# A gated S4 and feed-forward kernel: the order of the first projection's opening steps, with nine rounding steps moved between two engines

## The chip, the cores and the metric

The kernel runs on one NeuronCore of a Trainium2 chip. The metric is the device time of one execution in microseconds (us), the median of several runs. Five engines work side by side, each through its own list of instructions in order: TensorE (PE, with its weight loads as PEld), VectorE (DVE), ScalarE (ACT), GpSimd (POOL) and SyncE (SP, which here only issues transfers). They wait for one another through semaphores.

## The reference

The input `A_u` has 2048 rows of 512 features. It is normalized row by row, and two branches read the result:

```python
xn = _layernorm(x, axis=-1)
s = _A_ref(xn, A_re, A_im, B_re, B_im, C_re, C_im, log_dt, Dskip)   # S4: K from exp(dt*A*l), convolution by FFT
h = _gelu(xn @ w1 + b1)                                             # 512 -> 1792, tanh form
g = _silu(h @ w2 + b2)                                              # 1792 -> 512
return x + s * g
```

In `_A_ref` the parameters give for every feature a kernel `K` of 2048 taps as a sum over 128 states of complex exponentials. Everything is float32.

## The kernel before

**Tiling.** The feed-forward branch goes in steps `(v, f)`: `v` counts blocks of 512 rows (four blocks, visited twice, `v` 0 to 7), `f` counts 14 tiles of 128 hidden features, seven of them in each visit. Step number 0 to 55 stands in the names below. Each float32 matrix product is made of three fp32r products: a matrix is split into a rounded high part and a low remainder, and high times high, high times low and low times high are added up. `w1h`, `w1l`, `w2h`, `w2l` are the parts of the weights, `xh`, `xl` those of the normalized and transposed rows, `hh`, `hl` those of the gelu's result.

**One step** consists of the first projection (`first_half`, 12 matmuls with 512 columns, lines 255 to 257, in two halves; step 0 uses `first_start`, line 265), the gelu on ACT (`gate`, line 269), its rounded copy on ACT (`gate_high`, line 275), the remainder on DVE (`ffn_rest`, line 281) and the second projection (`second_part`, four quarters of three matmuls, lines 294 to 296; step 0 adds `b2` in two of the quarters with one more matmul each, line 293, from the tile `b2r`). The weights come by `stage_first` (a tile of `w1`, line 221) and `stage_second` (a tile of `w2`, line 226) into four rotating buffers; `split` makes the high parts on ACT (line 238) and the low parts on DVE or POOL (line 240).

**Beside it**, the S4 kernel `K` is generated in 32 subblocks. `params` computes on POOL, DVE and ACT the parameters of a quarter of the features (lines 499 to 574, with an arctan at line 520); `gen_phase` (PE, line 598) and `gen_round` (ACT, line 606, or DVE, line 608) and `gen_wrap` (DVE, line 612) make the phases, `gen_sin` the sines on ACT, `gen_size` the magnitudes on POOL (line 623), `gen_tables` the products on DVE (lines 646 to 653), and `gen_sum` sums them on PE (line 662, 128 small matmuls). `gen_round(s, h, other)` is on ACT where `h != other`, else on DVE.

**The order** is written by hand. `prologue()` loads the first rows, normalizes them (`ln_stats`, line 325, `ln_rsqrt`, lines 335 to 345, `ln_scale`, line 350), transposes them on PE (line 366), casts them on ACT (line 375) and DVE (line 381) and runs step 0's first projection. Ahead of the transposes PE runs 31 `warm` matmuls on an identity (line 432). Then a string `ORDER` of 1250 tokens is walked: `F.j.h` is half `h` of step `j`'s first projection, `G`, `H`, `R` its gelu, copy and remainder, `S.j.i` quarter `i` of its second projection, `W.f` and `WB.f` the loads of `w1` and `w2`, `WS.f.k` the splits (`k` 0 and 1 the high parts of `w1` and `w2`, 2 and 3 the low parts, on POOL where a 1 follows), `P.b` the next piece of `params(b)`, `LL`, `LS`, `LR`, `LC`, `LD` load, statistics, root, scaling and storing of later rows, `TF`, `TH`, `TL` their transposes, `A.s.h`, `B.s.h`, `C.s.h` phase, rounding and wrapping of subblock `s`, `Z`, `N`, `E`, `Q` magnitudes, sines, products and sums. Every engine gets its instructions in the order of these tokens, so a token that waits holds up everything later on the same engine.

The functions that the diff touches, and what calls them:

Of the kernel before, what the change touches and what calls it, by code (L numbers as in the profile page):

```python
# [48 lines left out]
WS.0.3 P.0 LD.0 P.0 P.0 WS.1.0 WS.1.1 WS.1.2 F.1.0 G.0 H.0 LD.1 W.2 R.0 WS.1.3 F.1.1 WS.2.0 LS.2.0 G.1  # L49
H.1 LS.3.1 LS.3.0 S.0.0 S.0.1 S.0.2 WB.2 WS.2.1 LL.4 WS.2.2 R.1 WS.2.3 LS.2.1 P.0 P.0 F.2.0 F.2.1 LL.5  # L50
W.3 WS.3.0 WB.3 W.4 WB.4 WS.3.1 WS.3.2 W.5 F.3.0 F.3.1 P.0 P.0 G.2 G.3 P.0 P.0 P.0 P.0 S.0.3 H.2 R.2 H.3
WS.4.0 WS.3.3 WS.4.1 WS.4.2 WS.5.0 LR.2 S.1.0 WB.5 LC.2 S.1.1 S.1.2 S.1.3 S.2.0 S.2.1 P.0 W.6 F.4.0
F.4.1 S.2.2 LC.3 S.2.3 KL.0.0 KL.0.1 G.4 H.4 R.3 TF.2.0 TH.2.0 KL.1.0 KL.1.1 S.3.0 Z.0 A.0.0 B.0.0.1
LS.5.0 R.4 TF.2.1 TH.2.1 BB S.3.1 TL.2.0 TF.3.0 WB.6 C.0.0 A.0.1 P.0 WS.5.1 WS.4.3.1 S.3.2 Z.1 TL.2.1
TH.3.0 B.0.1 WS.6.0 WS.5.2 F.5.0 TL.3.0 WS.6.1 C.0.1 N.0.0 N.0.1 TF.3.1 F.5.1 G.5 P.1 A.1.0 S.3.3 S.4.0
S.4.1 LS.4.0 LS.5.1 TH.3.1.1 B.1.0 C.1.0 A.1.1 B.1.1 TL.3.1 WS.6.2 S.4.2 S.4.3 H.5 E.0.0 LS.4.1 F.6.0
F.6.1 G.6 H.6 C.1.1 R.5 WS.5.3.1 S.5.0 LR.4 S.5.1 F.7.0 F.7.1 R.6 LC.5 LC.4 KL.2.0 KL.2.1 A.2.0 N.1.0
F.8.0 E.0.1 LK.0 S.5.2 S.5.3 N.1.1 F.8.1 LD.2 G.7 WS.6.3 E.0.2 E.1.0 B.2.0.1 G.8 H.7 LD.3 H.8 S.6.0
O.0.0 P.1 S.6.1 S.6.2 C.2.0 A.2.1 B.2.1 P.1 R.7 R.8 O.0.1 C.2.1 N.2.0 F.9.0 KL.3.0 F.9.1 KL.3.1 G.9
KL.4.0 A.3.0 E.1.1 E.1.2 S.6.3 S.7.0 TF.4.0 Z.2 P.1 Q.1 H.9 S.7.1 O.0.3 O.0.2 S.7.2 B.3.0.1 C.3.0 A.3.1  # L60
P.1 TH.4.0 TL.4.0 N.2.1 S.7.3 KL.4.1 TF.4.1 TH.4.1 R.9 F.10.0 F.10.1 B.3.1.1 S.8.0 Z.3 S.8.1 LD.5 C.3.1
N.3.0 N.3.1 G.10 H.10 E.2.0 A.4.0 KL.5.0 P.1 E.2.1 TL.4.1 E.2.2 B.4.0 C.4.0 R.10 F.11.0 F.11.1 G.11 H.11
S.8.2 E.3.0 S.8.3 S.9.0 R.11 E.3.1 E.3.2 LD.4 LL.6 TF.5.0 TH.5.0 U.1 A.4.1 TL.5.0 D B.4.1 F.12.0 F.12.1
G.12 H.12 S.9.1 C.4.1 S.9.2 LK.1 R.12 Z.4 UD.1 A.5.0 B.5.0.1 C.5.0 TF.5.1 TH.5.1 Q.3 P.1 LL.7 A.5.1 P.1
P.1 S.9.3 S.10.0 S.10.1 S.10.2 S.10.3 KL.6.0 KL.5.1 P.1 U.3 KL.6.1 B.5.1 C.5.1 LS.6.0 S.11.0 S.11.1
S.11.2 P.1 N.4.0 TL.5.1 P.1 F.13.0 F.13.1 LS.7.0 OK.0 N.4.1 E.4.0 S.11.3 N.5.0 N.5.1 UD.3 G.13 H.13 Z.5
S.12.0 E.4.1 E.4.2 E.5.0 S.12.1 A.6.0 LK.2 R.13 S.12.2 S.12.3 Z.6 B.6.0 F.14.0 F.14.1 C.6.0 A.6.1 LS.7.1
P.1 E.5.1 B.6.1 G.14 H.14 C.6.1 F.15.0 KL.7.0 E.5.2 F.15.1 P.2 A.7.0 G.15 LS.6.1 S.13.0 H.15 R.14 R.15
B.7.0.1 N.6.0 N.6.1 S.13.1 C.7.0 S.13.2 S.13.3 Q.5 A.7.1 P.1 F.16.0 F.16.1 B.7.1 F.17.0 F.17.1 LR.6 LC.6
LC.7 P.2 E.6.0 E.6.1 KL.8.0 O.1.0 S.14.0 E.6.2 C.7.1 O.1.2 O.1.1 S.14.1 G.16 H.16 S.14.2 G.17 H.17 N.7.0  # L70
# [1238 lines left out]
```

## Time and profile before

| | |
|---|---|
| time, median of 3 runs | 532.0 us (531.85 to 533.8) |
| profiled execution, its own time | 532.66 us |
| profiled execution, span | 530.8 us |
| granted TensorE clock | 0.997 |
| PE busy | 517.2 us (97%) |
| DVE busy | 428.5 us (81%) |
| ACT busy | 391.6 us (74%) |
| POOL busy | 258.5 us (49%) |

The span is that of the traced instructions; the execution's own time holds 1.86 us more. Times inside the profile are counted from the span's start. PE's busy time is that of pipelined matmuls, so what matters is where PE stood idle and who released it.

### The profile page before, as it was taken

The page shows a single profiled execution, that of the slowest core. Times are in us where ns is not written, and L with a number is a line of the kernel's source. Part 1 is how long each engine was busy: PE and PEld are TensorE (multiplying, and loading weights), DVE is VectorE, ACT ScalarE, POOL GpSimd, SP SyncE. Part 2 cuts the span into 40 slices and gives each one's busy share as a digit, 9 for nine tenths or more (in the row PEclk, how much of TensorE's full clock was granted, in tenths as well). Part 3 has the DMA queues.
Part 4 walks back from the last instruction along what each step waited for, and adds up shares of the span by engine and source line. Part 5 has one row for each costly group of instructions (what it writes and reads, how often), then busy time and mean ns, then how long its engine had stood idle before and what let it go on. Part 6 is the DMA issues. An engine that isn't in the chain of part 4 may idle for free.

```text
span 530.8 us, 16519 instructions
## 1 busy us (share of the span) xinstructions
PE 517.2 (97%) x6995; PEld 421.6 (79%) x6995; DVE 428.5 (81%) x726; ACT 391.6 (74%) x558; POOL 258.5 (49%) x384
## 2 busy tenths in 40 slices
PE   8899999999999999999999999999999999999995
PEld 7677778878777776877777777788889998998882
DVE  6998999999998789787875886898257779677896
ACT  3698896999987987988778799799464573663331
POOL 5629377657697478669818175635301002103041
PEclk9999999999999999999999999999999999999998
DMA  8937438752327974418135533590757539442562
GB/s 223 318 119 217 155 102 254 259 181 77 132 80 226 364 212 143 140 46 235 41 108 175 185 59 112 131 186 34 253 199 228 68 108 216 160 163 82 182 208 94
DMA packets 86087, 85.91 MB, mean 162 GB/s; under 512 B 41751, under 2 KB 60699, under 8 KB 84989
## 3 DMA queue, kind: packets, MB, share of 16 engines
q1 hardware_dynamic: 76944, 66.49, 42.5%
q0 software_dynamic: 8768, 17.83, 10.8%
q8 instruction: 55, 0.90, 0.7%
q10 hardware_dynamic: 300, 0.53, 0.3%
q14 instruction: 20, 0.16, 0.1%
HBM read 51.28 MB, written 33.55 MB: 160 GB/s over the span
## 4 chain that ended last, share of the span: by engine, by line
PE 84%; DVE 6%; ACT 3%; POOL 3%; issue 2%; DMA 2%; POOLq 0%; DVEq 0%; ACTq 0%
PE s L918 11%; PE z L294 9%; PE z L296 8%; PE z L295 8%; PE f L255 8%; PE f L257 8%; PE f L256 8%; PE s L896 6%; PE sa L955 6%; PE kg L662 5%; PE ph L598 3%; PE y L1014 2%; DMA w1s<-in_B_w_dram 1%; DVE hl L281 1%; PE xT L366 1%
## 5 line engine op out<-in xcount | busy, mean ns | idle before, releaser
L623 POOL TENSOR_TENSOR mm<-mm,rc 128x32 f32<-128x32 f32 (+4 forms) x150 | 97.1, 647 | 11.8
L294 PE MATMUL z<-w2h,hh 128*128 128x512 f32 x224 | 95.6, 427 | 0.0
L255 PE MATMUL f<-xh,w1h 128*128 128x512 f32 x220 | 91.6, 416 | 0.2 <-DVE hl L281 0.2
L257 PE MATMUL f<-xh,w1l 128*128 128x512 f32 x220 | 87.1, 396 | 2.8 <-DVE w1l L240 1.5
L296 PE MATMUL z<-w2h,hl 128*128 128x512 f32 x224 | 87.7, 391 | 0.1
L295 PE MATMUL z<-w2l,hh 128*128 128x512 f32 x224 | 87.7, 391 | 0.0
L256 PE MATMUL f<-xl,w1h 128*128 128x512 f32 x220 | 86.8, 395 | 0.0
L612 DVE SCALAR_TENSOR_TENSOR ra<-ra,ph 128x512 f32<-128x512 f32 x64 | 43.8, 684 | 19.6 <-ACT ra L606 18.7
L918 PE MATMUL s<-X,mc 64*64 64x128 f32 x1536 | 58.3, 272 | 0.8 <-DVE t L936 0.4
L936 DVE TENSOR_TENSOR t<-s,uh 128x512 f32<-128x512 f32 x64 | 40.9, 684 | 15.6 <-ACT uh L926 12.1
L269 ACT ACTIVATE f<-f,b1s 128x512 f32<-128x512 f32 x56 | 37.2, 665 | 19.3 <-PE f L257 18.0
L646 DVE TENSOR_TENSOR e<-mm,ra 128x1024 f32<-128x1024 f32 x32 | 43.3, 1355 | 10.1 <-ACT ra L634 4.3
L257 PEld LDWEIGHTS f<-xh,w1l 128*128 128x128 f32 x220 | 41.3, 188 | 12.2 <-DVE w1l L240 2.2
L255 PEld LDWEIGHTS f<-xh,w1h 128*128 128x128 f32 x220 | 41.5, 189 | 10.9 <-issue 1.5
L296 PEld LDWEIGHTS z<-w2h,hl 128*128 128x128 f32 x224 | 42.0, 188 | 10.2 <-DVE hl L281 0.5
L294 PEld LDWEIGHTS z<-w2h,hh 128*128 128x128 f32 x224 | 42.4, 189 | 9.0 <-issue 0.3
L620 POOL COPY mm<-rc 128x32 f32<-128x32 f32 x30 | 14.9, 496 | 71.0 <-DVE e L653 40.9
L918 PEld LDWEIGHTS s<-X,mc 64*64 64x64 f32 x1536 | 44.9, 133 | 5.8 <-issue 2.0
L926 ACT COPY uh<-s 128x512 f32<-128x512 f32 x32 | 18.8, 587 | 40.7 <-PE s L918 24.7
L295 PEld LDWEIGHTS z<-w2l,hh 128*128 128x128 f32 x224 | 42.2, 189 | 8.2
L256 PEld LDWEIGHTS f<-xl,w1h 128*128 128x128 f32 x220 | 41.4, 188 | 9.1
L281 DVE TENSOR_TENSOR hl<-f,hh 128x512 fp32r<-128x512 f32 x56 | 37.8, 682 | 10.6 <-ACT hh L275 10.6
(188 smaller groups left out, 1128.5 us busy)
## 6 DMA issues: line engine op xcount, KB each, us to landing
x<-in_A_u_dram SPq DMA_DIRECT2D x8, 512.0 KB
xs<-x SPq DMA_DIRECT2D x8, 512.0 KB
xt_h<-xh POOLq DMA_DIRECT2D x4, 1024.0 KB, 6.2
xt_l<-xl POOLq DMA_DIRECT2D x4, 1024.0 KB, 8.8
kgd<-ko SPq DMA_DIRECT2D x16, 256.0 KB
za<-zo SPq DMA_DIRECT2D x4, 1024.0 KB
xh<-xt_h POOLq DMA_DIRECT2D x4, 1024.0 KB, 6.6
xl<-xt_l POOLq DMA_DIRECT2D x4, 1024.0 KB, 9.3
```

The source lines that it names most:

```text
L255: PE.matmul(p, wh[:, k, :], xh[:, k, :], start=(k == 0), stop=False)
L256: PE.matmul(p, wh[:, k, :], xl[:, k, :], start=False, stop=False)
L257: PE.matmul(p, wl[:, k, :], xh[:, k, :], start=False, stop=(k == KD - 1))
L281: V.tensor_sub(hl, hf, hh)
L294: PE.matmul(z, hh[:, s], wh, start=(f0 == 0 and not rows), stop=False)
L295: PE.matmul(z, hh[:, s], wl, start=False, stop=False)
L296: PE.matmul(z, hl[:, s], wh, start=False, stop=(f0 == FA - 1))
L612: V.scalar_tensor_tensor(ra[:, 0, c], ra[:, 1, c], MAGIC, p, op0=ALU.subtract, op1=ALU.subtract)
L623: GP.tensor_mul(mv[:, :, 0:3:2, w:2 * w], mv[:, :, 0:3:2, 0:w], rc[:, 2 + 2 * i:4 + 2 * i, :].rearrange("p j c -> p c j").unsqueeze(3).to_ ...
L646: V.tensor_mul(e1, m1.unsqueeze(1).to_broadcast([P, 2, CH, N1]), ra[:, :, :, :N1])
L918: PE.matmul(p[ka * 64:(ka + 1) * 64, r, o, :, jj], w, xf[b][h, c, :, k, :], start=(c == 0), stop=(c == 1), skip_group_check=True)
L936: V.tensor_mul(t, p[:, i, :, 1].unsqueeze(1).to_broadcast([P, 2, 2, P]), uh)
```

## The change

It has three parts.

- `b2`'s low part. `bias_low()`, one DVE subtraction on one row (line 424), is taken out of the prologue, where it stood between the statistics of the first two row tiles, and becomes a token `BL`, placed behind the first half of step 1's first projection.
- The first 217 tokens of `ORDER` are written in another order, about a sixth of the string; none is lost. From the token `TL.4.0` on, the order is the old one.
- Nine roundings change their engine. 14.1, 19.0, 20.1, 22.0, 23.0 and 26.1 go from ACT to DVE, and 6.0, 27.1 and 28.1 go from DVE to ACT. DVE has 34 of the 64 roundings instead of 31.

```diff
 ORDER = """
-WS.0.3 P.0 LD.0 P.0 P.0 WS.1.0 WS.1.1 WS.1.2 F.1.0 G.0 H.0 LD.1 W.2 R.0 WS.1.3 F.1.1 WS.2.0 LS.2.0 G.1
-H.1 LS.3.1 LS.3.0 S.0.0 S.0.1 S.0.2 WB.2 WS.2.1 LL.4 WS.2.2 R.1 WS.2.3 LS.2.1 P.0 P.0 F.2.0 F.2.1 LL.5
+WS.1.0 WS.1.1 WS.0.3 WS.1.2 LD.0 LD.1 F.1.0 P.0 P.0 P.0 G.0 W.2 WB.2 W.3 BL F.1.1 H.0 R.0 S.0.0 S.0.1
+P.0 P.0 WS.1.3 WB.3 S.0.2 S.0.3 G.1 H.1 LS.2.0 LS.3.1 R.1 LS.3.0 WS.2.0 WS.2.1 WS.2.2 WS.2.3 S.1.0 F.2.0
...
-E.17.1 E.17.2 P.3 A.19.0 B.19.0.1 S.31.1 C.19.0 S.31.2 Q.17 A.19.1 P.3 R.33 B.19.1.1 KL.19.1 C.19.1
+E.17.0 N.18.0 H.34 E.17.1 E.17.2 P.3 A.19.0 B.19.0 S.31.1 C.19.0 S.31.2 Q.17 A.19.1 P.3 R.33 B.19.1.1
...
         ln_stats(0, mv[:, 0:2, :])
-        bias_low()
         ln_stats(1, mv[:, 2:4, :])
...
         "BB": bias_spread,
+        "BL": bias_low,
```

**ACT, from the end of the prologue on.** In the names, `w1h_340` (before) and `w1h_313` (now) are the high part of step 1's `w1`, `w1h_369` and `w1h_426` that of step 2, `pr_` tiles belong to `params(0)`, `f_0_1` is step 1's projection and `hh_0`, `hh_1` are the rounded gelus of steps 0 and 1. Before:

```order
L507 ACTIVATE pr_bi<-pr_wr 128x128
L508 ACTIVATE pr_cr<-pr_wi 128x128
L238 CAST w1h_340<-w1s_212 128x512
L238 CAST w2h_342<-w2s_214 128x512
L269 ACTIVATE f_0_0_301<-f_0_0_301,b1s 128x512
L275 CAST hh_0_355<-f_0_0_301 128x512
L238 CAST w1h_369<-w1s_358 128x512
L269 ACTIVATE f_0_1_347<-f_0_1_347,b1s 128x512
L275 CAST hh_1_380<-f_0_1_347 128x512
L238 CAST w2h_371<-w2s_403 128x512
L520 ACT_TABLE_LOAD
L520 ACTIVATE pr_cr<-pr_bi 128x128
```

Now:

```order
L238 CAST w1h_313<-w1s_212 128x512
L238 CAST w2h_315<-w2s_214 128x512
L507 ACTIVATE pr_bi<-pr_wr 128x128
L508 ACTIVATE pr_cr<-pr_wi 128x128
L269 ACTIVATE f_0_0_300<-f_0_0_300,b1s 128x512
L275 CAST hh_0_368<-f_0_0_300 128x512
L520 ACT_TABLE_LOAD
L520 ACTIVATE pr_cr<-pr_bi 128x128
L269 ACT_TABLE_LOAD
L269 ACTIVATE f_0_1_323<-f_0_1_323,b1s 128x512
L275 CAST hh_1_411<-f_0_1_323 128x512
L238 CAST w1h_426<-w1s_355 128x512
```

The casts of step 1's weights went ahead of the two parameter instructions; the arctan, with a table load on either side of it, went ahead of step 1's gelu; and the cast of step 2's `w1` went behind that gelu.

**DVE, behind the transposes of the first rows.** Here `w1l_341` and `w1l_314` are the low part of step 1's `w1`, `w2l_251` and `w2l_250` that of step 0's `w2`. Before:

```order
L240 TENSOR_TENSOR w2l_251<-w2s_137,w2h_250 128x512
L511 TENSOR_TENSOR pr_ci<-pr_bi,pr_cr 128x128
L512 TENSOR_TENSOR pr_br<-pr_bi,pr_cr 128x128
L513 TENSOR_TENSOR pr_m<-pr_cr,pr_bi 128x128
L515 TENSOR_SCALAR pr_bi<-pr_ci 128x128
L516 RECIPROCAL pr_bi<-pr_bi 128x128
L517 TENSOR_TENSOR pr_bi<-pr_bi,pr_br 128x128
L240 TENSOR_TENSOR w1l_341<-w1s_212,w1h_340 128x512
L281 TENSOR_TENSOR hl_0_360<-f_0_0_301,hh_0_355 128x512
```

Now:

```order
L240 TENSOR_TENSOR w2l_250<-w2s_137,w2h_249 128x512
L240 TENSOR_TENSOR w1l_314<-w1s_212,w1h_313 128x512
L511 TENSOR_TENSOR pr_ci<-pr_bi,pr_cr 128x128
L512 TENSOR_TENSOR pr_br<-pr_bi,pr_cr 128x128
L513 TENSOR_TENSOR pr_m<-pr_cr,pr_bi 128x128
L515 TENSOR_SCALAR pr_bi<-pr_ci 128x128
L516 RECIPROCAL pr_bi<-pr_bi 128x128
L517 TENSOR_TENSOR pr_bi<-pr_bi,pr_br 128x128
L424 TENSOR_TENSOR b2r<-b2st,b2r 1x512
L281 TENSOR_TENSOR hl_0_370<-f_0_0_300,hh_0_368 128x512
```

`w1l` of step 1 went ahead of the six parameter instructions, and `b2r` took its old place.

**DVE, a little later.** `w1l_370` (before) and `w1l_427` (now) are the low part of step 2's `w1`, `hl_1` is the remainder of step 1's gelu, `bst` and `mv` are statistics of rows. Before:

```order
L325 BN_STATS bst_0_385<-x_228 128x6
L326 BN_AGGR mv_374<-bst_0_385 128x2
L240 TENSOR_TENSOR w1l_370<-w1s_358,w1h_369 128x512
L281 TENSOR_TENSOR hl_1_409<-f_0_1_347,hh_1_380 128x512
L240 TENSOR_TENSOR w2l_372<-w2s_403,w2h_371 128x512
```

Now:

```order
L281 TENSOR_TENSOR hl_1_421<-f_0_1_323,hh_1_411 128x512
L325 BN_STATS bst_0_423<-x_228 128x6
L326 BN_AGGR mv_413<-bst_0_423 128x2
L240 TENSOR_TENSOR w1l_427<-w1s_355,w1h_426 128x512
L240 TENSOR_TENSOR w2l_429<-w2s_357,w2h_428 128x512
```

Step 2's `w1l` went behind step 1's remainder and one pair of statistics. Further on, the low part of step 3's `w1` (`WS.3.2`) stands behind the parameter instructions of lines 534 to 550, ahead of which it stood.

On SP the loads of row tiles 4 and 5 (`LL.4`, `LL.5`), which stood ahead of the loads of `w1` of step 3 and of all later ones, now stand behind `w1` and `w2` of steps 3 and 4.

More of the change, by code (lines that the diff above doesn't have):

```diff
@@ L54 @@
[L54 to L58, printed above, removed]
@@ new lines @@
+P.0 P.0 R.2 LR.2 WS.4.0 WS.3.3 WS.4.1 WS.4.2 F.3.1 S.2.0 LC.2 KL.0.0 S.2.1 S.2.2 S.2.3 WB.5 P.0 LS.5.0
+G.3 F.4.0 F.4.1 H.3 R.3 S.3.0 LS.4.0 A.0.0 WS.5.0 G.4 H.4 B.0.0.1 TF.2.0 R.4 TH.2.0 WS.5.1 WS.4.3.1
+C.0.0 W.6 S.3.1 S.3.2 KL.0.1 WB.6 WS.6.0 TF.2.1 BB TH.2.1 A.0.1 S.3.3 S.4.0 LC.3 KL.1.0 KL.1.1 P.0
+TL.2.0 TF.3.0 TL.2.1 S.4.1 Z.0 B.0.1 C.0.1 WS.5.2 WS.6.1 TH.3.0 WS.6.2 F.5.0 LS.5.1 N.0.0 N.0.1 TL.3.0
+P.1 A.1.0 S.4.2 TF.3.1 B.1.0 F.5.1 G.5 S.4.3 TH.3.1.1 TL.3.1 F.6.0 C.1.0 A.1.1 LS.4.1 E.0.0 H.5 R.5
@@ new lines @@
+A.23.0 B.23.0 S.39.1 S.39.2 N.22.0 N.22.1 S.39.3 S.40.0 C.23.0 A.23.1 B.23.1.1 KL.24.0 KL.25.0 S.40.1
+S.40.2 Q.21 U.21 C.23.1 N.23.0 S.40.3 R.42 E.22.0 E.22.1 Z.23 P.3 N.23.1 S.41.0 S.41.1 S.41.2 A.24.0
+E.22.2 B.24.0.1 F.43.0 E.23.0 F.43.1 C.24.0 G.43 H.43 A.24.1 B.24.1.1 C.24.1 F.44.0 F.44.1 R.43 G.44
+S.41.3 A.25.0 E.23.1 E.23.2 H.44 F.45.0 B.25.0.1 N.24.0 Q.23 C.25.0 A.25.1 R.44 ZL.1 F.45.1 F.46.0
+F.46.1 B.25.1.1 UD.21 KL.26.0 KL.24.1 N.24.1 ZA.1.2 ZA.1.1 ZA.1.3 ZA.1.0 KL.25.1 C.25.1 Z.24 E.24.0
@@ L126 @@
+E.29.2 ZA.2.2 UD.27 A.31.0 B.31.0 ST H.52 Q.29 C.31.0 A.31.1 ZA.2.3 S.49.2 S.49.3 G.53 S.50.0 Z.31
+N.30.0 B.31.1.1 S.50.1 R.52 F.54.0 F.54.1 C.31.1 S.50.2 N.30.1 H.53 E.30.0 S.50.3 U.29 S.51.0 S.51.1
+S.51.2 N.31.0 N.31.1 R.53 F.55.0 E.30.1 S.51.3 E.30.2 E.31.0 E.31.1 KL0 UD.29 S.52.0 S.52.1 F.55.1
+S.52.2 ZG.2 ZD.2 E.31.2 Q.31 S.52.3 S.53.0 S.53.1 S.53.2 S.53.3 G.54 U.31 G.55 H.54 H.55 R.54 R.55 UD.31
 """
```

129 lines of the change are left out of this document (60 added, 69 removed).

## The prediction

> **What bounds the kernel now.** I read first the busy shares on the page, then the list of what PE waited for over the whole span, then the timelines of the first 30 us engine by engine. The shares:
>
> ```profile
> PE 517.2 (97%) x6995; PEld 421.6 (79%) x6995; DVE 428.5 (81%) x726; ACT 391.6 (74%) x558; POOL 258.5 (49%) x384
> ```
>
> PE's waits, longest in total first (us in total, times, longest):
>
> ```profile
> PE f L257 <- DVE w1l L240: 1.5, 1, 1.5
> PE warm L432 <- POOL ident masks.py:199: 1.5, 1, 1.5
> PE f L257 <- issue: 1.3, 1, 1.3
> PE f L265 <- ACT xh L375: 0.7, 1, 0.7
> PE xT L366 <- DVE x L350: 0.5, 1, 0.5
> PE ph L598 <- DVE ra L612: 0.4, 2, 0.2
> ...
> PE xT L366 <- DVE hl L281: 0.2, 1, 0.2
> PE f L255 <- DVE hl L281: 0.2, 1, 0.2
> ```
>
> PE sets the end: it is busy 97% of the span, and its matmuls are the same ones before and after. So a new order is worth just what it takes from PE's waits or adds to them. The change rewrites the front of the kernel, where the first wait lies (step 1's third matmul, 1.5 us for `w1l`) and the 0.5 us ahead of the transposes. PE's timeline there (start, duration, engine, line; in brackets the idle time ahead and its releaser):
>
> ```profile
> 4.56 6.31 PE L432 MATMUL warm<-ident 128*128 128x128 f32 x50
> 11.38 2.17 PE L366 MATMUL xT<-ident,x 128*128 128x128 f32 x16 [0.52 <-DVE x L350]
> 14.22 1.20 PE L265 MATMUL f<-xh,w1h 128*128 128x512 f32 x4 [0.67 <-ACT xh L375]
> ...
> 17.13 0.40 PE L255 MATMUL f<-xh,w1h 128*128 128x512 f32 x1
> ...
> 19.29 0.50 PE L257 MATMUL f<-xh,w1l 128*128 128x512 f32 x1 [1.53 <-DVE w1l L240]
> ...
> 21.73 0.40 PE L293 MATMUL z<-b2r,ones 128*128 128x512 f32 x1
> ```
>
> DVE's:
>
> ```profile
> 6.07 0.18 DVE L326 BATCH_NORM_AGGREGATE mv<-bst 128x2 f32<-128x6 f32 x1
> 6.44 0.70 DVE L424 TENSOR_TENSOR b2r<-b2st,b2r 1x512 fp32r<-1x512 f32 x1 [0.20 <-ACT b2r L421]
> 7.17 0.69 DVE L325 BATCH_NORM_STATS2 bst<-x 128x6 f32<-128x512 f32 x1
> ...
> 10.78 2.06 DVE L350 TENSOR_SCALAR x<-x,mv,rs 128x512 f32<-128x512 f32 x4
> ...
> 15.77 0.68 DVE L240 TENSOR_TENSOR w2l<-w2s,w2h 128x512 fp32r<-128x512 f32 x1
> 16.37 0.28 DVE L511 TENSOR_TENSOR pr_ci<-pr_bi,pr_cr 128x128 f32<-128x128 f32 x1
> ...
> 18.34 0.29 DVE L517 TENSOR_TENSOR pr_bi<-pr_bi,pr_br 128x128 f32<-128x128 f32 x1
> 18.55 0.68 DVE L240 TENSOR_TENSOR w1l<-w1s,w1h 128x512 fp32r<-128x512 f32 x1
> 19.15 0.68 DVE L281 TENSOR_TENSOR hl<-f,hh 128x512 fp32r<-128x512 f32 x1
> ```
>
> And ACT's:
>
> ```profile
> 12.08 2.09 ACT L375 CAST xh<-xT 128x512 fp32r<-128x512 f32 x4 [3.64 <-PE xT L366]
> ...
> 15.55 0.31 ACT L508 ACTIVATE pr_cr<-pr_wi 128x128 f32<-128x128 f32 x1 [1.10 <-POOL pr_wi L504]
> ...
> 17.32 0.66 ACT L269 ACTIVATE f<-f,b1s 128x512 f32<-128x512 f32 x1 [0.43 <-PE f L265]
> 18.02 0.59 ACT L275 CAST hh<-f 128x512 fp32r<-128x512 f32 x1
> 20.77 0.62 ACT L238 CAST w1h<-w1s 128x512 fp32r<-128x512 f32 x1 [2.17 <-DMA w1s<-in_B_w_dram]
> ```
>
> Step 1's `w1l` (DVE, 18.55) is late because six parameter instructions, 16.37 to 18.6, stand ahead of it; and those hang on ACT's line 508, which got `pr_wi` from POOL only at 15.55.
>
> **The change part by part.** PE's pace: ten matmuls from 19.29 to 21.73, 0.24 us each with the refill behind the wait; I use 0.233 for an undisturbed one. Two DVE instructions on 512 columns start 0.60 apart (18.55, 19.15).
>
> *1. `b2r` leaves the first statistics.* It cost DVE the time from 6.17 to 7.17, its own wait included. That is 1.0 us if the second row tile had landed by 6.17; the trace shows only that it had by 7.17, so 0 to 1.0, and I take 1.0. Scaling then starts at 9.78 for 10.78 and its first quarter is done at 10.3. But PE's warm matmuls end at 4.56 + 6.31 = 10.87 whatever DVE does, so the transposes gain only 0.5, and with them the casts (11.6 to 13.7) and step 0's projection (13.74 for 14.22). DVE's low parts follow the casts: `w2l` of step 0 at 15.27 for 15.77.
>
> *2. Step 1's weights ahead of the parameters.* `w1h` is now cast right behind ACT's casts, 13.7 to 14.3. `w1l` follows `w2l` at 15.27 + 0.60 = 15.87 and ends at 16.55. Step 1 starts at 17.13 - 0.48 = 16.65 and wants `w1l` two matmuls later, at 17.1: it is there. The matmul goes at 17.1 instead of 19.29, **-2.2 us**, which holds both the 1.5 and the 0.5.
>
> *3. What is late next.* Ten matmuls on, at 19.44, PE wants `b2r`. DVE's parameters now run from 16.47 to 18.7 and `b2r` behind them to 19.35: no wait, with 0.1 to spare. `hl` of step 0 starts at 19.25 and is wanted at 20.14: no wait. Where this cover fails, each costs what it is late by, some tenths.
>
> *4. Step 2's low part.* ACT now runs the arctan, between two table loads, ahead of step 1's gelu. Both kinds of row:
>
> ```profile
> 23.74 1.28 ACT L520 ACT_TABLE_LOAD   x1
> 25.04 0.31 ACT L520 ACTIVATE pr_cr<-pr_bi 128x128 f32<-128x128 f32 x1
> ```
>
> `hh` of step 0 ends at 18.02 + 0.59 - 0.48 = 18.1; load, arctan and load take 1.30 + 0.31 + 1.30, so the gelu starts at 21.05, and the cast behind it runs from 21.75 to 22.35. DVE waits for that cast: `hl` of step 1 from 22.4, a pair of statistics (0.8) from 23.0, step 2's `w1l` from 23.8 to 24.5. PE: fourteen matmuls of step 0 from 19.44 to 22.7, three of step 1 to 23.4, and the third of step 2, at 23.87, finds `w1l` 0.6 us away. This wait is new: **+0.6**, from 0 (ACT or DVE some tenths ahead) to 1.2.
>
> The Trainium skill, "ScalarE: Activation LUTs", section "What ACT_TABLE_LOAD costs", puts a switch of tables at 1.28 us for the load and 1.38 more for a drain; by it this term would be an estimated 3.4 instead of 0.6. The trace disagrees: the arctan starts 0.02 us after its load ends, with no drain between.
>
> *5. Step 3's low part* now stands behind thirteen parameter instructions, which wait for POOL's line 531. POOL's row, and DVE's first and last of the thirteen:
>
> ```profile
> 25.21 0.46 POOL L531 TENSOR_TENSOR pr_br<-pr_br,pr_m 128x128 f32<-128x128 f32 x1
> ```
>
> ```profile
> 27.33 0.34 DVE L534 SCALAR_TENSOR_TENSOR pr_ci<-pr_ci,sm_dt,pr_br 128x128 f32<-128x128 f32 x1
> ...
> 30.29 0.28 DVE L550 SCALAR_TENSOR_TENSOR xp<-pr_ai,pr_cr 128x128 f32<-128x128 f32 x1
> ```
>
> POOL's chain starts from DVE's line 517, now 0.1 later, so it ends at 25.8. The thirteen take 30.57 - 27.33 = 3.24, to 29.1, and step 3's `w1l` is ready at 29.75. PE finishes step 2's first half at 25.4, nine matmuls of step 1 at 27.5, the other half at 28.9, and wants that `w1l` at 29.4: **+0.4**, from 0 to 0.8.
>
> *6. The later transposes'* wait of 0.2 came from a remainder that stood behind four scalings on DVE; in the new order two of the four come behind it: **-0.2**, from 0 on.
>
> *7. Loads.* The cast of step 2's `w1` waited for its load until 20.77. In the new order it comes behind step 1's gelu, at 22.4, so the weights' earlier place on SP is worth nothing. Row tiles 4 and 5 (1 MB) are now issued when step 2's buffers are free, some 25 to 26.5, and DVE wants them only behind step 3's low parts, after 35. The rate in that stretch, the last column in GB/s:
>
> ```profile
> 20.00:30.00 10.00, 10.00 (x45) 7.90 (x44) 8.57 (x24) 7.18 (x10) 5.12 (x12) 1.00 0.74 243
> ```
>
> 1 MB takes 4.3 us at 243 GB/s: 0. If they were later than 35, DVE would stop ahead of step 3's remainder and PE behind it.
>
> *8. Roundings.* DVE's rows of that kind (ns, least, median and most), and the chain of waits where number 19.0 now comes, ahead of line 612:
>
> ```profile
> L608 DVE TENSOR_SCALAR ra<-ph x31: 671/691/693, 47.2 to 361.3; 128x512 f32<-128x512 f32 x31
> ```
>
> ```profile
> 239.54 0.60 DVE ra L612
> 240.13 0.61 DVE hl L281
> ...
> 240.79 0.50 PE f L255
> ```
>
> PE already waits here for the remainder, so one more DVE instruction ahead of both, 0.6 apart like its neighbours, is **+0.6**. At the other eight places PE has next to no wait, and I take 0; the five that go to DVE could cost 0.6 each (+3.0), and the three that leave it take no listed wait away.
>
> Sum: -2.2 + 0.6 + 0.4 - 0.2 + 0.6 = -0.8. The profiled execution took 532.66, so its like would take 531.9; the median of the runs shown, 532.0, is 0.66 below it, which gives **531.2**. The terms' own bounds make this 530.0 to 532.3.
>
> **The rivals.** *Faster, slack everywhere*: the waits of 4 and 5 are sums of many small gaps and may not come, and the chain ahead of 19.0 may have room. Then -2.2 - 0.2 = -2.4: 529.6. Against it: both waits come out of rows that can be followed one by one.
>
> *Faster still*: as that one, and the 1.3 us that PE waited for "issue", with no releaser, go as well, because what feeds PE there comes at another moment: -3.7, 528.3. For it: there is only one such wait of that size. Against it: nothing shows that the change reaches it.
>
> *Slower, DVE as the bound*:
>
> ```profile
> 100.00:120.00 20.00, 19.59 (x35) 1.00 0.73 229
> ```
>
> From 100 to 120 us DVE is busy 19.59 of 20. If its work sets the pace there, the lead is spent by 120, and the six roundings that DVE takes over later stand on the path at 0.61 each: +3.7, 535.7. It decides from the point where line 612 ends after PE wants the next phase. For it: that share. Against it: PE waited for line 612 only twice, 0.4 in all.
>
> *Slower, dearer table switches*: if each of the two switches that now stand ahead of step 1's gelu held ACT for twice the 1.28 us of the load's row, term 4 would be 0.6 + 2.6 = 3.2: 533.8. The two rows of term 4 speak against it, since the arctan starts right behind its load. This is what the section of the Trainium skill named in term 4 would have.
>
> That the change doesn't do what it says is excluded by the order of the instructions.
>
> **How the numbers follow.** Forecast 0.40, slack everywhere 0.22, faster still 0.18, DVE as the bound 0.17, dearer switches 0.03. A measurement of this kernel tells about 0.5% (2.66 us) from no change, so the bounds are 529.3 and 534.7. Faster: 0.17 from the fastest case, 0.08 from the lower third of slack, 0.01 from the forecast, 0.26. Slower: 0.17, DVE as the bound. Within: 0.57. The range leaves out the lower end of the fastest case and the slower bound: 528.5 to 534.2.
>
> **What would show it.** Right: transposes from 10.9 and step 1's third matmul near 17.1, with no wait for its `w1l`; new waits of PE for `w1l` near 24 and 29; step 5's second projection 1.4 us earlier than before; a wait of about 0.8 near 239. Wrong: none of these waits (slack), a missing "issue" wait, or waits of PE for line 612 in many places (DVE as the bound).

## The result, and the profile after

The changed kernel takes 534.08 us (median of 14 runs, 533.07 to 536.54), the kernel before 532.84 (14 runs, 531.05 to 534.18). The ratio is 1.0028, 95% interval 1.0014 to 1.0041: slower by 0.7 to 2.2 us, where 531.2 and no measurable change were forecast. The profiled execution took 535.34 us, its span 533.5.

Busy shares of the changed kernel, and what PE waited for (us in total, times, longest):

```profile
PE 519.1 (97%) x6995; PEld 422.0 (79%) x6995; DVE 432.5 (81%) x729; ACT 389.1 (73%) x555; POOL 260.4 (49%) x384
```

```profile
...
PE f L255 <- issue: 1.3, 1, 1.3
PE ph L598 <- DVE ra L612: 1.1, 2, 0.9
PE s L918 <- issue: 1.0, 1, 1.0
...
PE f L257 <- DVE w1l L240: 0.6, 2, 0.3
PE f L255 <- DVE hl L281: 0.4, 2, 0.2
...
PE xT L366 <- DVE xl L381: 0.4, 1, 0.4
```

The wait of 1.5 for `w1l` is gone; two of 0.3 for `w1l`, one of 0.4 for `xl`, and 0.7 more for line 612 are new. PE's timeline in the front of the changed kernel:

```profile
4.56 6.73 PE L432 MATMUL warm<-ident 128*128 128x128 f32 x50
11.13 1.91 PE L366 MATMUL xT<-ident,x 128*128 128x128 f32 x16
13.87 1.20 PE L265 MATMUL f<-xh,w1h 128*128 128x512 f32 x4 [0.83 <-ACT xh L375]
...
17.24 0.39 PE L257 MATMUL f<-xh,w1l 128*128 128x512 f32 x1
...
19.69 0.50 PE L293 MATMUL z<-b2r,ones 128*128 128x512 f32 x1
...
24.69 0.50 PE L257 MATMUL f<-xh,w1l 128*128 128x512 f32 x1 [0.34 <-DVE w1l L240]
...
30.12 0.50 PE L257 MATMUL f<-xh,w1l 128*128 128x512 f32 x1 [0.30 <-DVE w1l L240]
...
43.92 0.66 PE L366 MATMUL xT<-ident,x 128*128 128x128 f32 x4 [0.40 <-DVE xl L381]
```

Step 1's third matmul starts 2.05 us earlier (17.24 for 19.29). A wait costs about 0.25 more than its idle time: matmuls that follow one another start 0.23 apart and last 0.39, so they overlap by 0.16, and a wait takes this overlap away; and the second matmul behind a wait starts 0.34 behind the first (24.69 and 25.03). I call this the refill.

To follow that lead I take the times at which PE begins one of its sums (line 662, a group of 128 small matmuls that every kernel runs in the same order), as a difference to the first profile of before (69.99, 136.76, 238.01 and 263.41 us). The first of these marks lies close to the end of the rewritten tokens, the second behind them, the others on either side of the roundings 19.0 and 20.1. Each ratio compares with runs of the kernel before on the same chip.

| kernel | at 70 | at 137 | at 238 | at 263 | median (runs) | ratio to before, 95% interval |
|---|---|---|---|---|---|---|
| before, profiled twice | 0, +0.83 | 0, +1.02 | 0, +0.44 | 0, +0.46 | | |
| changed, profiled twice | -0.47, -0.30 | +0.05, +0.20 | +0.15, -0.77 | +1.45, +0.54 | 534.08 (14) | 1.0028, 1.0014 to 1.0041 |
| changed, old engines, twice | -0.90, -0.50 | -0.44, -0.07 | -0.33, -0.26 | -0.32, -0.27 | 531.99 (12) | 0.9976, 0.9959 to 0.9993 |
| changed, 19.0 and 20.1 back | -0.96 | -0.54 | -1.29 | -1.28 | 532.78 (12) | 0.9978, 0.9963 to 0.9994 |
| before, nine roundings | +0.29 | +0.48 | +0.52 | +1.85 | 535.65 (12) | 1.0033, 1.0011 to 1.0056 |
| before, 19.0 alone | +0.23 | +0.67 | +0.07 | +0.79 | 533.36 (1) | |
| before, 20.1 alone | +0.31 | +0.57 | +0.52 | +0.52 | 532.21 (1) | |
| before, step 1 alone | -0.42 | -0.25 | -0.20 | -0.20 | 534.72 (12) | 1.0027, 1.0007 to 1.0047 |

The old front was profiled five times (before twice, and the three kernels with roundings alone): mean +0.33 at 70 and +0.55 at 137. The new front too (changed, and old engines, twice each, and the two back): -0.63 and -0.16. So **the new front gains 1.0 us at 70 and 0.7 at 137**; single pairs say anything from 0.3 to 1.8 at 70, and from -0.2 to 1.6 at 137.

Much of this scatter is there before 15 us. Step 0's projection (line 265) starts between 13.20 and 13.87 us in the five profiles of the new front (mean 13.58) and between 14.13 and 14.67 in those of the old one (mean 14.41). Counted from that start, step 1's third matmul comes after 3.37 to 3.43 us in the new front and after 5.03 to 5.07 in the old, so the weights' new place is worth 1.7 us there. But the sum near 70 us comes after 55.65 to 55.86 us in the new front and after 55.56 to 55.92 in the old (56.69 in the one execution that waited for a late load). **So by 70 us nothing is left of the 1.7 us.** What the front keeps is step 0's earlier start, 0.8 us, and ahead of step 0 only `b2r` has changed its place; the rest of the 1.0 is that late load in the old front's mean.

And wherever both 19.0 and 20.1 are on DVE, **PE loses 1.3 us between 238 and 263** (1.30, 1.31, 1.33); elsewhere 0.0, and 0.7 with 19.0 alone.

### The profile page after: what moved, and what is told of

The parts are those of the page before. It is cut to its first block, busy times and chain, and to the rows that moved or that the text cites. A ratio compares the mean times of both kernels' runs of the same rounds, so it can differ in the third digit from the quotient of the medians.

```text
span 533.5 us, 16513 instructions
## 1 busy us (share of the span) xinstructions
PE 519.1 (97%) x6995; PEld 422.0 (79%) x6995; DVE 432.5 (81%) x729; ACT 389.1 (73%) x555; POOL 260.4 (49%) x384
## 4 chain that ended last, share of the span: by engine, by line
PE 87%; DVE 7%; issue 2%; ACT 2%; POOL 1%; DVEq 0%; POOLq 0%; ACTq 0%
PE s L918 11%; PE z L294 9%; PE f L255 9%; PE z L295 9%; PE z L296 9%; PE f L257 9%; PE f L256 8%; PE s L896 6%; PE sa L955 6%; PE kg L662 5%; PE ph L598 3%; PE warm L432 2%; PE y L1014 2%; PE xT L366 1%; DVE hl L281 1%
## 5 line engine op out<-in xcount | busy, mean ns | idle before, releaser
L623 POOL TENSOR_TENSOR mm<-mm,rc 128x32 f32<-128x32 f32 (+4 forms) x150 | 99.9, 666 | 11.8
L646 DVE TENSOR_TENSOR e<-mm,ra 128x1024 f32<-128x1024 f32 x32 | 42.1, 1317 | 9.4 <-ACT ra L634 3.7
L620 POOL COPY mm<-rc 128x32 f32<-128x32 f32 x30 | 13.5, 449 | 70.7 <-DVE e L653 39.3
```

What stands on the lines that cost most here:

```text
L623: GP.tensor_mul(mv[:, :, 0:3:2, w:2 * w], mv[:, :, 0:3:2, 0:w], rc[:, 2 + 2 * i:4 + 2 * i, :].rearrange("p j c -> p c j").unsqueeze(3).to_ ...
L646: V.tensor_mul(e1, m1.unsqueeze(1).to_broadcast([P, 2, CH, N1]), ra[:, :, :, :N1])
```

## The experiments

### The roundings: four kernels that take the change apart

All on one chip, with before at 533.72 us. The changed kernel with all nine roundings on their old engines:

```diff
-B.6.0.1 B.14.1.1 B.19.0 B.20.1.1 B.22.0 B.23.0 B.26.1.1 B.27.1 B.28.1
+B.6.0 B.14.1 B.19.0.1 B.20.1 B.22.0.1 B.23.0.1 B.26.1 B.27.1.1 B.28.1.1
```

> The changed kernel with all nine roundings back on their old engines; its new order of the front stays. Theory R (the roundings that went to DVE cost PE about 0.7 us near 240 and 0.6 us near 262, and the front's lead is used up by 131 us): as fast as the kernel before, within 0.3 us, and no wait of PE for line 612 above 0.3 us near 240. Rival F (the loss sits in the new front, or in PE's waits with no releaser): still about 1.2 us slower than before.

The kernel before with those nine lines of the change alone (the diff above, reversed):

> The kernel before with nothing but the nine roundings moved. Theory R: 1.2 to 1.4 us slower than before, with PE's waits for line 612 near 240 and for line 281 near 262 grown by 0.6 to 0.7 us each, and nothing at the other seven places. Rival F: the same as before within 0.3 us.

The changed kernel with two of them back:

```diff
-B.19.0 ... B.20.1.1
+B.19.0.1 ... B.20.1
```

> The changed kernel with only roundings 19.0 and 20.1 put back on ACT. Theory R in its narrow form (these two alone cost): the same as with all nine back, so within 0.3 us of the kernel before. If the other four that went to DVE cost too, it stays 0.5 us or more slower than with all nine back. Rival F: 1.2 us slower than before.

The kernel before with the reordering of step 1 alone:

```diff
-WS.0.3 P.0 LD.0 P.0 P.0 WS.1.0 WS.1.1 WS.1.2 F.1.0
+WS.1.0 WS.1.1 WS.0.3 WS.1.2 P.0 LD.0 P.0 P.0 BL F.1.0
```

> The kernel before with part of the new front alone: b2r's low part out of the first statistics, and step 1's weight splits ahead of the parameter pieces. Theory G (a lead of PE is given back at the next DVE or ACT result that is late): step 1's third matmul at 17.2 instead of 19.3, but step 2's then waits 1.3 to 1.7 us for its low part and step 3's waits for its weights, which land at 26, so that the first sums (70.0 in the kernel before) come at most 0.5 us earlier and the time is within 0.5 us of before. Rival L (a lead lasts): the first sums come 2 us earlier and the time is 1.5 to 2.2 us below before.

The first three agree: the front alone makes the kernel faster (0.9976), the roundings alone make it slower (1.0033), and two of the nine carry that (0.9978 with these two back). Theory R had the two places right but not the front: it expected the first and the third kernel within 0.3 us of before, and their ratios put them 1.3 and 1.2 us below it. The fourth doesn't fit: its profiled execution was its quickest (531.03 us, PE 0.2 to 0.4 ahead), its ratio to before 1.0027. Its step 2 has a wait of its own, in its PE timeline:

```profile
24.32 0.50 PE L257 MATMUL f<-xh,w1l 128*128 128x512 f32 x1 [1.16 <-DVE w1l L240]
```

so most of step 1's gain is lost at once (1.16 and the refill, of 1.7); why it is slower than before stays open.

### 19.0 and 20.1, one at a time, and two repeats

```diff
-B.19.0.1
+B.19.0
```

> The kernel before, with the rounding 19.0 alone moved from ACT to DVE. If each of the two places costs by itself what the trace of the changed kernel shows: PE's wait for line 612 near 240 us grows from 0.2 to 0.9, PE is 0.6 to 0.7 us late against before from 241 us on, and nothing more is added at 263 us. If the wait is DVE's backlog of several moved roundings: 0.2 or less here.

```diff
-B.20.1
+B.20.1.1
```

> The kernel before, with the rounding 20.1 alone moved from ACT to DVE. If it costs by itself: PE waits 0.6 us near 263 us for a remainder and stays that late. If it cost only because 19.0 had already put DVE behind: 0.2 or less.

The kernel before and the changed kernel once more, with no edit:

> The kernel before, unchanged, profiled once more, to see how far two executions of one kernel differ. If PE's waits without a releaser (1.3 us near 204 us, 0.3 near 450 us) belong to the program, they stand where they stood, within 0.1 us; if they belong to the execution, they differ by as much as between the kernels, up to 1.3 us, and the times at which PE reaches the same instruction differ by some tenths before 70 us too.

> The changed kernel once more, to size the difference between two executions of it. Marks of PE at 70 us within 0.5 us of the first profile, the waits near 240 and 263 us (0.7 and 0.6 of delay) there again within 0.15; the waits without a releaser near 205 and 450 us anywhere from 0 to 1.3.

19.0 costs 0.72 by itself. 20.1 costs nothing by itself and 0.6 behind 19.0. DVE's timeline from 20.1 (its first row) to the remainder that PE waits for, then POOL's, in the changed kernel:

```profile
255.54 0.69 DVE L608 TENSOR_SCALAR ra<-ph 128x512 f32<-128x512 f32 x1 [0.76 <-PE ph L598]
...
256.75 1.22 DVE L650 TENSOR_TENSOR e<-mm,ra 128x1024 f32<-128x1024 f32 x1
...
258.48 1.10 DVE L652 TENSOR_TENSOR e<-mm,ra 128x512 f32<-128x512 f32 x1
259.50 1.60 DVE L653 SCALAR_TENSOR_TENSOR e<-mm,ra 128x512 f32<-128x512 f32 x1
...
262.54 0.68 DVE L281 TENSOR_TENSOR hl<-f,hh 128x512 fp32r<-128x512 f32 x1
```

```profile
256.13 4.42 POOL L623 TENSOR_TENSOR mm<-mm,rc 128x32 f32<-128x32 f32 x5
```

The same with 20.1 alone:

```profile
255.20 0.69 DVE L608 TENSOR_SCALAR ra<-ph 128x512 f32<-128x512 f32 x1 [0.76 <-PE ph L598]
...
256.41 1.35 DVE L650 TENSOR_TENSOR e<-mm,ra 128x1024 f32<-128x1024 f32 x1
...
258.28 0.77 DVE L652 TENSOR_TENSOR e<-mm,ra 128x512 f32<-128x512 f32 x1
258.98 1.15 DVE L653 SCALAR_TENSOR_TENSOR e<-mm,ra 128x512 f32<-128x512 f32 x1
...
261.57 0.68 DVE L281 TENSOR_TENSOR hl<-f,hh 128x512 fp32r<-128x512 f32 x1
```

```profile
256.38 4.72 POOL L623 TENSOR_TENSOR mm<-mm,rc 128x32 f32<-128x32 f32 x5
```

With 20.1 alone that `hl` is just in time: PE's line 255 starts at 262.31, 0.10 us behind the matmul of line 598 (0.04 in the kernel before). In the changed kernel lines 652 and 653 last 2.70 instead of 1.92 beside POOL, `hl` starts 0.97 later, and PE is held by 0.6. DVE was not behind when these lines began: measured from PE's matmul of line 598 (259.54 and 259.20), 20.1 starts 4.00 us ahead in both kernels. What differs is POOL, whose line 623 starts 3.41 ahead of that matmul in the changed kernel and 2.82 with 20.1 alone. Counted from the sum near 238 us, that matmul comes 0.7 later behind 19.0 and POOL's line 623 only 0.1: 19.0 had put PE and DVE back, not POOL, and so the two lines met POOL's work at another moment. Their durations are the same (1.10 and 1.59 or 1.60) in the other two profiles with both roundings on DVE. PE's rows in the changed kernel:

```profile
262.68 0.39 PE L598 MATMUL ph<-cbs,lh 96*128 96x512 bf16 x1
263.27 0.50 PE L255 MATMUL f<-xh,w1h 128*128 128x512 f32 x1 [0.21 <-DVE hl L281]
```

The repeats show both delays again (1.31 in sum). They show also that two executions of the kernel before differ by 3.5 us of span (530.8 and 534.3), 3.0 of it behind 376 us: PE's waits without a releaser were 0.7 for 1.3 near 205 us and more numerous behind 440 us, and a late load cost 0.7 at 27.8 us:

```profile
PE s L918 <- issue: 1.7, 4, 0.7
...
PE f L257 <- issue: 0.7, 1, 0.7
PE f L255 <- ACT w1h L238: 0.7, 1, 0.7
```

The changed kernel's second execution has a wait that the first has not, 0.97 us in all, between its sums at 359.52 and 377.27. None of the nine roundings lies there. Lines 652 and 653 ahead of it last 2.69 instead of 1.62 (0.68 and 0.94 in the first execution): POOL's line 623 starts 1.34 ahead of DVE's line 650 there, and 0.27 behind it in the first execution, where it had waited for a load. PE's row and DVE's:

```profile
362.42 0.39 PE L598 MATMUL ph<-cbs,lh 96*128 96x512 bf16 x1 [0.82 <-DVE ra L612]
```

```profile
357.82 1.10 DVE L652 TENSOR_TENSOR e<-mm,ra 128x512 f32<-128x512 f32 x1
358.85 1.59 DVE L653 SCALAR_TENSOR_TENSOR e<-mm,ra 128x512 f32<-128x512 f32 x1
```

So the same program can lose a microsecond or not, by how DVE's and POOL's instructions meet in that execution.

### Where the lead of step 1 went

Two theories: the lead is lost to separate waits, each of which can be taken away; or DVE, busy for 25.41 of the 27 us from 18 to 45 in the changed kernel, sets PE's pace. The kernels of this section start from the changed one with the old engines, two from the kernel before. First, both waits for `w1l` taken away by the order, and by an arctan of the first parameter set that comes a piece later:

```diff
-S.0.0 S.0.1 P.0 P.0 WS.1.3 ... G.1 H.1 LS.2.0 LS.3.1 R.1 LS.3.0 WS.2.0 WS.2.1 WS.2.2 WS.2.3 ...
+S.0.0 S.0.1 P.0 WS.1.3 ... WS.2.0 G.1 H.1 WS.2.2 LS.2.0 R.1 LS.3.1 LS.3.0 WS.2.1 P.0 WS.2.3 ...
-W.4 LS.2.1 S.1.3 P.0 P.0 WS.3.0 WS.3.1 F.2.1 G.2 WS.3.2 F.3.0
+W.4 LS.2.1 S.1.3 WS.3.0 WS.3.2 P.0 P.0 WS.3.1 F.2.1 G.2 F.3.0
...
-        A.activation(an, q, AF.Arctan)
-        yield
+        if b: A.activation(an, q, AF.Arctan)
+        if b: yield
...
         GP.tensor_mul(y, y, sq)
         yield
+        if not b: A.activation(an, q, AF.Arctan); yield
```

> The new order's front with the nine roundings on their old engines, and with two more edits that take away the two waits that PE has in the changed kernel for the low parts of step 2 (24.69 us) and of step 3 (30.12 us): of the first parameter set the arctan on ACT comes behind its chain on POOL and behind the casts of step 2's weights, so that step 1's gelu and step 2's low part come earlier; and the low part of step 3's w1 comes ahead of the parameter instructions of lines 534 to 550. All the work is done. Theory 'two waits': the lead of 2.2 us that PE has at step 1 was lost to these two waits and a few others of 0.2 to 0.6 each, and each can be taken away by itself; then PE is 1.1 us further ahead than in the kernel with the old engines, -1.6 to -2.0 at 70 us and at 137 us, and the time falls by 1 us more, ratio to before near 0.995. Rival 'DVE sets the pace': DVE is busy without a gap from 18 to 45 us, so what it does earlier for one step it does later for the next; the two waits go and as much comes back between 36 and 137 us: PE stands within 0.3 us of the kernel with the old engines from 70 us on, ratio 0.9976 as there.

Both waits went, and PE stood at +2.56 at 70 us; the ratio is 1.0043 (1.0022 to 1.0065). More came back than was taken, in PE's timeline:

```profile
34.57 0.50 PE L296 MATMUL z<-w2h,hl 128*128 128x512 f32 x1 [1.95 <-DVE hl L281]
...
38.35 0.50 PE L257 MATMUL f<-xh,w1l 128*128 128x512 f32 x1 [0.75 <-DVE w1l L240]
```

Neither theory forecast a loss. DVE's parameter instructions (line 534 on) start 1.6 us later than with the old engines alone (27.40 for 25.79), and three of DVE's instructions now lie beside POOL's: one of line 556 lasts 1.39 for 0.43, and the two scalings of line 350 last 2.53 together for 1.16.

Then work taken off DVE: two low parts given to POOL; or five instructions left out in the new and in the old order.

```diff
-WS.2.3 ... WS.3.3
+WS.2.3.1 ... WS.3.3.1
```

> The new order with the nine roundings on their old engines, and with the low parts of w2 of steps 2 and 3 on POOL instead of DVE (two DVE instructions of 0.6 us less between 24 and 36 us; POOL had about 10 us free there). All the work is done. DVE sets the pace from 18 to 45 us: PE is 0.6 to 1.2 us further ahead than with the old engines alone, so at 70 us it stands at -1.4 to -2.0 on the scale on which that kernel stands at -0.9, at 137 us at -1.0 or better if the lead lasts; ratio near 0.995. Contention outweighs it: POOL's two instructions lie beside DVE's parameter instructions and slow them by as much as they relieve DVE of, as they did in the last kernel (0.43 to 1.39); no gain, ratio 0.9976 or higher.

```diff
+        if b == 0: GP.memset(pc, 0.0)
-        for i in range(3):
+        for i in range(3 if b else 0):
```

> The new order with the nine roundings on their old engines, and of the first parameter set the five DVE instructions of lines 554 and 556 (1.8 us, from 30.0 to 31.8) are left out, replaced by one memset on POOL: that part of the computation is missing, so only the time of the rest counts. DVE sets the pace: the waits of PE behind 32 us (0.2 at 36, 0.6 at 44, 0.4 behind it) shrink, PE is 0.8 to 1.8 us further ahead at 70 us than with the old engines alone, -1.7 to -2.5. Each wait is its own: no more than 0.3 further ahead.

> The kernel before with the same five DVE instructions left out (lines 554 and 556 of the first parameter set, so this part of the computation is missing). If DVE sets the pace in the old order too, PE gains 0.8 to 1.8 us there as well and stands at -0.5 to -1.5 at 70 us where the kernel before stands at 0 to 0.8; then what DVE has to do up to 45 us, and not the order, holds both. If the old order is held by its own waits (step 1's low part), PE gains no more than 0.3.

With 1.8 us less for DVE, PE stood at -0.83 at 70 us in the new order (-0.90 and -0.50 without the edit) and at +0.35 in the old (mean +0.33): nothing gained; ratios 0.9978 (0.9960 to 0.9997) and 0.9988 (0.9967 to 1.0010). DVE idled instead, waiting for two transposes of PE:

```profile
29.21 0.68 DVE L240 TENSOR_TENSOR w1l<-w1s,w1h 128x512 fp32r<-128x512 f32 x1
31.40 0.29 DVE L569 COPY al<-pT 128x128 f32<-128x128 f32 x1 [1.50 <-PE pT L566]
```

So up to there DVE's sum of work doesn't set the pace. Behind 31.4 us this test says little, since DVE goes on at the old time. The two low parts on POOL made it worse: +2.35 at 70 us, ratio 1.0046 (1.0028 to 1.0063). POOL's timeline and DVE's:

```profile
25.46 1.30 POOL L240 TENSOR_TENSOR w2l<-w2s,w2h 128x512 fp32r<-128x512 f32 x1
...
26.86 1.29 POOL L240 TENSOR_TENSOR w2l<-w2s,w2h 128x512 fp32r<-128x512 f32 x1
```

```profile
25.54 1.37 DVE L534 SCALAR_TENSOR_TENSOR pr_ci<-pr_ci,sm_dt,pr_br 128x128 f32<-128x128 f32 x1 [0.46 <-POOL pr_br L531]
26.83 1.40 DVE L535 TENSOR_SCALAR pr_ar<-pr_ar,sm_dt 128x128 f32<-128x128 f32 x1
```

Line 534 lasted 1.37 for 0.35 and line 535 1.40 for 0.28; they end 0.15 and 0.08 us behind POOL's. I call this a meeting. PE idled 2.14 us for step 3's `w1l`, which stands behind them. The changed kernel has such a meeting ahead of its wait at 43.92. Its DVE, then its POOL:

```profile
35.98 1.16 DVE L350 TENSOR_SCALAR x<-x,mv,rs 128x512 f32<-128x512 f32 x2
...
41.27 2.00 DVE L350 TENSOR_SCALAR x<-x,mv,rs 128x512 f32<-128x512 f32 x2
```

```profile
41.69 1.29 POOL L240 TENSOR_TENSOR w2l<-w2s,w2h 128x512 fp32r<-128x512 f32 x1 [1.69 <-ACT w2h L238]
```

Two pairs of scalings of one shape took 1.16 and 2.00. So this POOL instruction was moved to DVE, and its base run once more beside it:

```diff
-WS.5.3.1
+WS.5.3
```

> The new order with the nine roundings on their old engines, and one more edit: the low part of step 5's w2 (line 240, 1.30 us on POOL from 41.27 us) goes to DVE, a good ten us later, where PE waits for nothing. All the work is done. DVE and POOL hold each other up: in the kernel with the old engines the two scalings of line 350 at 40.84 took 2.01 us instead of 1.16 because they met this POOL instruction; without it DVE's low parts of the transposed rows come 0.5 to 0.8 earlier, the wait of PE at 43.5 us (0.4, 0.56 with the refill) goes, and PE stands at -1.4 to -1.8 at 70 us where it stood at -0.9; ratio 0.996 to 0.997. DVE's sum of work decides: it has 0.6 more to do and PE stands at -0.3 to -0.9 at 70 us; ratio 0.998 or more.

> The new order with the nine roundings on their old engines, once more, as the base of the run beside it: PE within 0.4 us of its first profile at 70 us (-0.9), the wait at 43.5 us there again with 0.4 us.

The scalings took 1.16 and the wait at 43.5 us went, as forecast by the meetings; but POOL's next work now came 3 us earlier and met DVE's next low parts (2.24 for 1.38), and PE waited 0.78 at 47.34. It also waited 0.49 at 53.84 for the moved low part itself, where the expectation had seen no wait. DVE's timeline of this run:

```profile
40.78 1.16 DVE L350 TENSOR_SCALAR x<-x,mv,rs 128x512 f32<-128x512 f32 x2
...
43.65 2.24 DVE L240 TENSOR_TENSOR w1l<-w1s,w1h 128x512 fp32r<-128x512 f32 x2
```

PE stood at -0.18 at 70 us; ratio 1.0005 (0.9986 to 1.0024). The base, run once more, stood at -0.50 and had its wait of 0.40. Last, POOL's magnitudes of two subblocks left out on top of this, and in the old order:

```diff
+        if s < 2: GP.memset(mm, 0.0); gen[s]["mm"] = mm; return
```

> The kernel of the run before last (new order, old engines, the low part of step 5's w2 on DVE), and the magnitudes of the first two subblocks (POOL, lines 620 to 625, some 4.8 us each) replaced by one POOL memset each: that part of the computation is left out. From 36 to 50 us DVE now meets hardly any POOL instruction that reads SBUF. If the meetings took the lead back: line 240's pair at 43.65 takes 1.38 instead of 2.24, the wait of 0.8 at 47.3 us goes, and PE stands at -0.9 to -1.4 at 70 us, where the kernel without this edit stood at -0.2. If not: within 0.4 of -0.2.

> The kernel before with the same two pieces of POOL's work replaced by memsets (left out, as there). In the old order DVE lost only 0.6 us to meetings between 32 and 45 us and PE had no wait behind them but 0.4 at 39.5 and 0.4 at 54.3 us; so if the meetings matter only for the new order PE stands at 0 to 0.8 at 70 us, as in the executions of the kernel before; if POOL's work slows both orders alike, at -0.4 to -1.2.

This test failed in its aim and showed the mechanism at its plainest. Behind 38 us the pair of line 240 took 1.29 and the wait at 47.3 us was gone, as expected. But the memset and two DMA issues on POOL now fell on two DVE instructions of four columns, and PE waited 2.60 us at 39.30 for the low part behind them: +2.82 at 70 us, ratio 1.0058 (1.0029 to 1.0088); in the old order +1.45, 1.0010 (0.9994 to 1.0026), with new waits of 0.87 and 0.65. POOL and DVE in the new order:

```profile
33.59 1.39 POOL L619 MEMSET mm<- 128x1536 f32 x1
34.91 0.98 POOL L385 DMA_DIRECT2D xt_h<-xh  x1
35.90 0.77 POOL L386 DMA_DIRECT2D xt_l<-xl  x1
```

```profile
33.31 1.70 DVE L335 TENSOR_SCALAR va<-mv,eps 128x4 f32<-128x4 f32 x1
35.04 1.63 DVE L336 TENSOR_SCALAR rs<-va 128x4 int32<-128x4 int32 x1
```

In the changed kernel these two lasted 0.39 and 0.17.

How much lead would be left with no meeting at all was therefore not measured.

Of the versions that do all the work, the changed kernel with the nine roundings on their old engines, 0.9976 (0.9959 to 0.9993), and the one with only 19.0 and 20.1 back, 0.9978 (0.9963 to 0.9994), are the best, faster than before and than the changed kernel.

## Why the prediction was wrong

| step of the prediction | forecast | measured |
|---|---|---|
| 1: transposes at | 10.9 | 11.13; 10.37 to 11.13 in the new front's five profiles (its 50 warm matmuls lasted 5.85 to 6.73) |
| 2: step 1's third matmul | 17.1 | 17.24 |
| 3: `b2r` | 0 | 0.2 (matmul at 19.69, wanted at 19.57) |
| 4: step 2's `w1l` | +0.6 | +0.6 (idle 0.34 and refill) |
| 5: step 3's `w1l` | +0.4 | +0.6 (idle 0.30 and refill) |
| 6: transposes | -0.2 | -0.5 (idle 0.24 and refill gone) |
| no term: wait at 43.92 | 0 | +0.6 (idle 0.40 and refill) |
| front, sum | -1.4 | -1.0 at 70 us, -0.7 at 137 (means of five) |
| 8: 19.0 | +0.6 | +0.7 |
| 8: 20.1 | 0 | +0.6 behind 19.0, 0 alone |
| 8: the other seven | 0 | 0 (ratio 0.9976 without and 0.9978 with them; from 263 us to the sum near 376 us PE takes 112.4 us either way) |

**Two steps failed, by about 0.7 us each. The first is term 8's "At the other eight places PE has next to no wait, and I take 0".** It was taken place by place, with the durations of the trace of before. At 20.1 alone it holds: the rounding uses up the slack there and PE loses nothing. But 19.0 puts PE and DVE back against POOL, the lines 652 and 653 meet POOL's line 623 at another moment and last 0.78 longer, and PE loses 0.6. 19.0 itself was sized a little low (0.7 for 0.6: line 612 starts 0.71 behind the new line 608). The bound of +3.0 for such places was written down, but it went neither into the likeliest case nor into the bounds of the sum. (Those bounds come out of the other terms as 530.2 and 532.4, not 530.0 and 532.3, and higher with term 1 at its least.)

**The second is the sum for the front: -1.4 forecast, -1.0 at 70 us and -0.7 at 137.** The lead was read rightly: step 0 starts 0.8 earlier (forecast 0.5), step 1's third matmul a further 1.7 earlier (forecast 1.7). What failed is how much of it comes back: 0.6 + 0.4 - 0.2 = 0.8 was forecast, and the rows above give 0.2 + 0.6 + 0.6 - 0.5 + 0.6 = 1.5 by 44 us, nearly the whole 1.7. The term that was missing is the last: DVE's durations were taken as fixed, though in a new order its instructions meet other POOL instructions. The meeting at 41.27 us cost PE these 0.6; between 70 and 137 us another 0.25 went, for which no run gives the cause. Dear switches of tables were rightly given little: in the changed kernel, too, the arctan starts 0.01 us behind its load on ACT:

```profile
18.27 1.28 ACT L520 ACT_TABLE_LOAD   x1
19.56 0.31 ACT L520 ACTIVATE pr_cr<-pr_bi 128x128 f32<-128x128 f32 x1
```

The rival "DVE as the bound" had the right sign for a wrong reason: seven of the nine roundings cost nothing, and with the lead in front of 120 us lost to single waits, no stretch is left that DVE's share would explain. The rival "faster still" counted on the wait without a releaser near 205 us: it was 1.29 and 0.72 in two executions of the kernel before, 1.27 and 0.22 in two of the changed one, so it belongs to the execution and not to the change. The mechanism is a few single instructions that come too late.

**What stays open.** The marks give -0.7 + 1.3 = +0.6 us; the ratio gives +1.5 (0.7 to 2.2). The rest may lie in PE's waits without a releaser, which differed by more than that between two executions of one kernel, or in meetings that come in some executions only, like the 0.97 us near 362 us; how often they come no run tells.

## What to carry to other kernels

Instructions that move to a busy engine should be costed together, not place by place against the trace of before: one of them shifts two engines against a third, and the next finds other neighbours. When an order changes, list which VectorE instructions will now lie beside which GpSimd instructions, and price each meeting that stands ahead of something TensorE waits for at up to the whole GpSimd instruction. And before explaining a difference of 1 us in 530 by two profiles, profile one of the two kernels twice, and count the times from a point behind the part that varies: here 0.7 us of difference between executions was there before step 0 began.

## What the hardware showed that was not expected

DVE and POOL hold each other up, but not with every instruction. Over the changed kernel (least, median and most, in ns):

```profile
L281 DVE TENSOR_TENSOR hl<-f,hh x56: 658/684/693, 19.7 to 381.6; 128x512 fp32r<-128x512 f32 x56
```

```profile
L612 DVE SCALAR_TENSOR_TENSOR ra<-ra,ph x64: 669/686/690, 40.7 to 364.0; 128x512 f32<-128x512 f32 x64
```

```profile
L652 DVE TENSOR_TENSOR e<-mm,ra x32: 677/686/1460, 59.6 to 373.2; 128x512 f32<-128x512 f32 x32
```

```profile
L350 DVE TENSOR_SCALAR x<-x,mv,rs x16: 539/544/1544, 9.8 to 117.1; 128x512 f32<-128x512 f32 x16
```

Lines 281 and 612 take one input from a tile that PE has just written (`f`, `ph`) and never last over 0.693 us, whatever POOL does; line 652, of the same size with both inputs in SBUF, reaches 1.46, and line 350, a scaling within SBUF, 1.54. The Trainium skill, "SBUF — State Buffer", section "Who interferes with whom", has this as a rule: DVE and GpSimd share one pair of ports, a DVE instruction with two SBUF inputs meets a GpSimd instruction that reads SBUF, one in a two-port mode meets any, and the second to issue is blocked until the first is done. The rows of lines 281, 612 and 652 agree with it. Line 350, and lines 335 and 336 above, which took 1.3 and 1.5 us longer beside a memset and DMA issues, have one tensor as input; they agree if they run in that two-port mode, which no row here shows. The prediction had not weighed that rule; with it, the new order's meetings could have been a term of the sum.
